# Attention on one core: the queries of eight heads loaded together in rows of 3 KB and put in place by GpSimd

## Chip, cores and metric

One core of a Trainium2 chip runs the kernel alone. The metric is the device time of one execution in microseconds (us), taken as the median of several executions. The engines are TensorE (PE; its weight loads are listed as PEld), VectorE (DVE), ScalarE (ACT), GpSimd (POOL) and SyncE (SP, which issues DMAs). DMA transfers run on 16 DMA engines that all queues share.

## What is computed

Softmax attention for 16 x 32 = 512 heads, each with 192 queries and 1024 keys of 128 numbers, all bf16:

```python
B, H, Sq, Sk, D = 16, 32, 192, 1024, 128
scale = q.shape[-1] ** -0.5
scores = jnp.einsum("bhqd,bhkd->bhqk", q, k) * scale
p = _softmax(scores, axis=-1)
return jnp.einsum("bhqk,bhkd->bhqd", p, v)
```

K and V are 134 MB each, Q and the output 25 MB each; every byte is moved once.

## The kernel before

**Tiling.** The heads are taken four at a time: 128 *quads*. Head a of a quad sits in partitions 32a to 32a+31, and its 128 contraction values are spread over these 32 partitions and four accumulating matmuls. The scores of a quad are computed transposed (keys on partitions) as 1536 columns: 8 key tiles of 192 queries. They are cut into three *steps* of 512 columns, so the program has NF = 384 steps f, with quad x = f // 3 and b = f % 3.

**One step.** TensorE computes QK of step f (line 654), then PV of step f-4 (line 683, `LAG = 4`). ScalarE takes the exp of head 0 (line 838) and of heads 1 to 3 (line 841) into `pt`. No maximum is subtracted. V has a column of ones beside it in `vp`, so PV gives the row sums too; VectorE takes their reciprocals (line 768) and multiplies (line 772) into `ob`. ScalarE's queue stores two quads at a time (line 522). A second, careful path stands behind a check of the row sums and isn't entered on this data.

**How Q, K and V get in place.** SP issues the loads, in an order written out by hand: for each n, V of quad n+3, K of quad n+5, Q of quad n+5. `load_k` (line 546) moves 128 rows of 8 KB, `load_v` (line 555) 512 rows of 2 KB, `load_q` (line 531) 128 rows of 1.5 KB (32 partitions per head, 6 query rows in each). K and V have five buffers each (`NKN`, `NVS`), and Q five (`qn`). SP waits until VectorE has turned K of quad n before it reuses the buffer, and until PV is done with V of quad n-2. The wait for K covers Q's buffer too.

VectorE turns K in three pieces per quad (`turn_k`, line 747) into `kx`, in 32 x 32 blocks of 4-byte words, three steps ahead (`AHEAD = 3`). GpSimd copies each piece into the order that TensorE reads (`order`, line 607, into `kt`). Q takes a shorter way: `turn_q` (line 756) turns it on VectorE with an output pattern that puts it in `qt` directly; it stands in VectorE's queue ahead of the K piece with b = 2. GpSimd also copies V into its padded place (`spread`, line 616), between the first and second K piece of the next quad. `qt`, `kt`, `vp` and `pt` have two buffers each, used in turn.

**Who waits for whom.** TensorE counts semaphores down (`take`). Ahead of QK it takes one of `s_kt` (GpSimd's K piece), one of `s_e1` (the exp that frees the scores' bank) and, at b = 0, one of `s_qt` (VectorE's Q). Ahead of PV it takes one of `s_on` (VectorE's last normalising step). V has no wait of its own in the loop: the K piece that follows `spread` in GpSimd's queue vouches for it.

Of the kernel before, what the change touches and what calls it, by code (L numbers as in the profile page):

```python
# [407 lines left out]
U32 = mybir.dt.uint32  # L408
# [12 lines left out]
def _attention_kernel(nc, q, k, v, out):  # L421
# [4 lines left out]
    NQ = NH // 4  # L426
    T = SK // 128
    scale = float(D) ** -0.5
    R = PE_LOOP
    assert NH % 8 == 0 and NQ >= 12  # L430
    NF = 3 * NQ
    LAG = 4
# [3 lines left out]

    AHEAD = 3
    NKN, NVS, NKT, NVP = 5, 5, 2, 2
    GQ = 2
    NSO = 3  # L440
    VB = 136
# [9 lines left out]
    with ExitStack() as outer:  # L451
# [7 lines left out]
        s_out = sem("f_out")  # L459
        s_blank = sem("f_blank")  # L460
        s_kn = [sem("f_kn%d" % i) for i in range(NKN)]
        s_qn = [sem("f_qn%d" % i) for i in range(NKN)]
        s_v = [sem("f_v%d" % i) for i in range(NVS)]
        s_st = [sem("f_st%d" % i) for i in range(NSO)]
        s_kx = sem("f_kx")
        s_qt = sem("f_qt")
        s_kt = sem("f_kt")
        s_vp = sem("f_vp")
        s_qk = sem("f_qk")
# [10 lines left out]
        with ExitStack() as es:  # L480
# [9 lines left out]
            kx = sb("f_kx", [128, 2, 2048], U32)  # L490

            kt = sb("f_kt", [128, NKT, 2 * T, 128, 2], BF16)
            qn = sb("f_qn", [128, NKN, 384], U32)

            qt = sb("f_qt", [128, R, 2, SQ, 2], BF16)
            vs = sb("f_vs", [128, NVS, 4, T * D], BF16)
# [32 lines left out]

            def load_q(e, x):  # L530
                e.dma_start(
                    qn[:, x % NKN, :],
                    qf[4 * x:4 * x + 4].rearrange("a (j u) d -> (a j) (u d)", u=6).bitcast(U32),
                ).then_inc(s_qn[x % NKN], 16)

            hints = {}

# [3 lines left out]
            @block.sync  # L541
            def _(e):
                def load_k(x, lo=0, hi=32):
                    if x >= NKN:
                        e.wait_ge(s_kx, 3 * (x - NKN) + 3)
                    e.dma_start(
                        kn[:, x % NKN, 64 * lo:64 * hi],
                        kf[4 * x:4 * x + 4].rearrange("a (j r) d -> (a j) r d", r=32)[:, lo:hi, :]
                        .rearrange("p r d -> p (r d)").bitcast(U32),
                    ).then_inc(s_kn[x % NKN], 16)  # L550

                def load_v(x, lo=0, hi=4):
                    if x >= NVS:
                        e.wait_ge(s_pv, 3 * (x - NVS) + 2 + BLANK)
                    e.dma_start(
                        vs[:, x % NVS, lo:hi, :],
                        vf[4 * x + lo:4 * x + hi].rearrange("a (m t) d -> m a (t d)", t=T),
                    ).then_inc(s_v[x % NVS], 16)


                load_k(0)
                e.wait_ge(s_blank, 1)
                load_k(1)
                load_q(e, 1)
                load_v(0, 0, 2)
                e.wait_ge(s_qk, PRE + 1)
                load_v(0, 2, 4)
                load_k(2, 0, 16)
                e.wait_ge(s_pv, BLANK - 2)
                load_k(2, 16, 32)  # L570
                load_q(e, 2)
                for n in range(3, NKN):
                    load_v(n - 2)
                    load_k(n)
                    load_q(e, n)
                for n in range(NQ):
                    if n == NQ // 2:
                        hint(e)
                    if n + NKN - 2 < NQ:
                        load_v(n + NKN - 2)  # L580
                    if n + NKN < NQ:
                        load_k(n + NKN)
                        load_q(e, n + NKN)
                for i in range(len(store_at), len(stores)):
                    store(e, i)
            def stored(e):
# [3 lines left out]
            @block.gpsimd  # L590
            def _(gp):
                gp.memset(ones[:], 1.0).then_inc(s_one, 1)  # L592

                def set_v(part):
                    return gp.memset(part.bitcast(U32), 0x3F803F80)  # L595

                set_v(vp[:, 0, 0:2 * T].rearrange("p a d -> p (a d)")).then_inc(s_set, 1)
                set_v(vp[:, 0, 2 * T:].rearrange("p a d -> p (a d)")).then_inc(s_blank, 1)
                set_v(vp[:, 1].rearrange("p a d -> p (a d)"))

                def order(g):
                    x, b = divmod(g, 3)
                    lo, hi = PIECES[b]
                    gp.wait_ge(s_kx, g + 1)
                    if x >= NKT - 1 and b == 0:
                        gp.wait_ge(s_qk, 3 * (x - NKT) + 3 + PRE)
                    gp.tensor_copy(  # L607
                        kt[:, x % NKT].bitcast(U32).rearrange("p U (j s u) c -> p U j s (u c)", s=2, u=2)[:, lo:hi],
                        kx[:, x % 2].rearrange("p (U s j u) -> p U j s u", s=2, j=32, u=2)[:, lo:hi],
                    ).then_inc(s_kt, 1)  # L610

                def spread(x, i):
                    if i == 0:
                        gp.wait_ge(s_v[x % NVS], 16 * (x // NVS + (2 if x % NVS == 0 else 1)))
                        gp.wait_ge(s_pv, 3 * (x - NVP) + 3 + BLANK)
                    gp.tensor_copy(  # L616
                        vp[:, x % NVP, 2 * T * i: 2 * T * i + 2 * T, 0:D].bitcast(U32),
                        vs[:, x % NVS, 2 * i: 2 * i + 2, :].rearrange("p a (t d) -> p (a t) d", d=D).bitcast(U32),
                    ).then_inc(s_vp, 1)

                for x in range(NQ + 1):
                    if x == NQ // 2:
                        hint(gp)
                    if x < NQ:
                        order(3 * x)
                    if x >= 1:
                        for i in range(2):
                            spread(x - 1, i)
                    if x < NQ:
                        order(3 * x + 1)  # L630
                        order(3 * x + 2)

            @block.tensor
            def _(pe):
# [3 lines left out]

                def qk(f):
                    x, b = divmod(f, 3)  # L640
                    if b == 0:
                        take(s_qt, 1)
                    take(s_kt, 1)
                    take(s_e1, 1)
                    ins = None
                    for group in CUTS[b]:
                        for w in range(4):
                            h, c = divmod(w, 2)
                            for g, (t, n0, n1) in enumerate(group):
                                c0 = t * SQ + n0 - 512 * b  # L650
                                for a in range(4):
                                    S = s3_ps[f % 2][:, a - 1, :] if a else s1_ps[:]
                                    r = slice(32 * a, 32 * a + 32)
                                    ins = pe.matmul(  # L654
                                        S[:, c0: c0 + n1 - n0],
                                        kt[r, x % NKT, 2 * t + h, :, c],
                                        qt[r, x % R, h, n0:n1, c],
                                        start=w == 0 and g == 0, stop=w == 3, skip_group_check=True,
                                        tile_position=(32 * a, 0))
                    ins.then_inc(s_qk, 1)  # L660
# [57 lines left out]
            def _(dve):  # L718
# [5 lines left out]
                    ins = clear(low[:, z, :, 1, :])  # L724
                ins.then_inc(s_set, 1)
                clear(qt[:, 1].rearrange("p h q c -> p (h q c)"))
                dve.sem_inc(s_e1, 1 + PRE)
                clear(kt[:, 1, 10:16].rearrange("p U k c -> p (U k c)")).then_inc(s_kt, 1)
                for z in range(2):
                    ins = clear(low[:, z, :, 2, :])  # L730
                ins.then_inc(s_out, 1)
                dve.wait_ge(s_out, 2)
                dve.wait_ge(s_blank, 1)
                dve.sem_inc(s_on, LAG + 1 + PRE)
                where = {}
                for i, (x0, c) in enumerate(stores):
                    for a in range(c):
# [2 lines left out]
                def turn_k(g):  # L740
# [8 lines left out]
                        kn[:, x % NKN].rearrange("p (s u U i) -> p s u U i", s=2, u=2, i=32)[:, :, :, lo:hi],  # L749
                    ).then_inc(s_kx, 1)  # L750

                def turn_q(x):
                    dve.wait_ge(s_qn[x % NKN], 16 * (x // NKN + 1))
                    if x >= R - 1:
                        dve.wait_ge(s_qk, 3 * (x - R) + 3 + PRE)
                    dve.transpose(  # L756
                        qt[:, x % R].bitcast(U32).rearrange("p b (y j u) c -> p u y b (j c)", y=3, u=2),
                        qn[:, x % NKN].rearrange("p (u y b i) -> p u y b i", u=2, y=3, b=2),
                    ).then_inc(s_qt, 1)

                def onorm(s):
                    x, w = divmod(s, 3)
# [35 lines left out]
                for f in range(NF + LAG + 1):  # L798
                    s = f - LAG - 1
                    if f == NF // 2:  # L800
                        hint(dve)
                    if s >= 0:
                        onorm(s)
                        if 0 <= s - EARLY < 3:
                            check(0, 2 * EARLY, 0, s - EARLY)
                    g = f + AHEAD
                    if 5 <= g < NF:
                        x, b = divmod(g, 3)
                        if b == 2 and x >= 2:
                            turn_q(x)  # L810
                        turn_k(g)
                for part in range(3):
                    check(2 * EARLY, 2 * NF, 1, part)
# [70 lines left out]
```

## Time and profile before

| what | value |
|---|---|
| median of 3 runs | 817.86 us (817.03 to 821.01) |
| profiled execution | 816.7 us, its span 815.0 us |
| granted TensorE clock | 0.996 |
| DMA over the span | 319.16 MB, mean 392 GB/s, 138455 packets (7217 under 512 B, 56369 under 2 KB) |
| ScalarE exps, lines 841 and 838 | 384 of 1444 ns and 384 of 597 ns |
| VectorE turns of K, line 747 | 256 of 972 ns (768 words), 128 of 670 ns (512 words) |
| VectorE turns of Q, line 756 | 128 of 570 ns (384 words) |
| GpSimd copies of K, line 607 | 256 of 863 ns (768 words), 128 of 642 ns (512 words) |
| GpSimd copies of V, line 616 | 256 of 1046 ns (1024 words) |
| issues of Q on SP, line 531 | 127, median 575 ns each |

The profile gives each engine's busy time over the span, and the groups of instructions by line, with the mean duration of one and the engine's idle time just before them. Busy times can overlap on one engine[...]. The *DMA share* is the time that packets took, as a share of 16 engines' time; the records of single packets lie in the trace. *Idle before* an instruction is put down to what released it last.

### The profile page before, as it was taken

What the parts mean: (1) busy time and instruction counts of PE and PEld (TensorE: products, weight loads), DVE (VectorE), ACT (ScalarE), POOL (GpSimd) and SP (SyncE); (2) the same over time, 40 slices, a digit from 0 to 9 for tenths busy, and PEclk for the clock granted to TensorE, in tenths of its full rate; (3) what the DMA queues carried; (4) which work ended last, traced back from release to release, by engine and by line L of the source; (5) the groups of instructions that cost most, each with busy time, mean ns of one, the idle gap of its engine ahead of it and who ended that gap; (6) DMA issues with size and microseconds to landing.
All of it is one profiled execution on the core that took longest, in us unless ns stands there. A gap on an engine that the chain in (4) does not pass through costs nothing. (4 is left out here: it accounts for less than half of the span.)

```text
span 815.0 us, 71454 instructions
## 1 busy us (share of the span) xinstructions
PE 802.2 (98%) x32996; PEld 716.0 (88%) x32996; DVE 602.0 (74%) x1293; ACT 749.9 (92%) x772; POOL 553.8 (68%) x648
## 2 busy tenths in 40 slices
PE   8899999999999999999999999999999999999997
PEld 7788888888888888888888888888888888888886
DVE  4677777777777777777777777777777777777775
ACT  6799999999999999999999999999999999999995
POOL 5677677667667766766676676676766766766674
PEclk9999999999999999999999999999999999999999
DMA  7999999999999999999999999999999999999992
GB/s 270 396 401 406 408 404 405 409 403 406 409 403 406 408 403 407 407 405 407 407 403 408 407 404 408 406 406 405 407 406 401 396 409 393 388 406 399 393 379 73
DMA packets 138455, 319.16 MB, mean 392 GB/s; under 512 B 7217, under 2 KB 56369, under 8 KB 122161
## 3 DMA queue, kind: packets, MB, share of 16 engines
q1 hardware_dynamic: 105536, 294.22, 91.9%
q10 hardware_dynamic: 32880, 24.58, 9.0%
q14 instruction: 33, 0.26, 0.1%
q8 instruction: 6, 0.10, 0.1%
HBM read 293.60 MB, written 25.17 MB: 391 GB/s over the span
## 5 line engine op out<-in xcount | busy, mean ns | idle before, releaser
L841 ACT ACTIVATE f_pt<-f_s 128x1536 bf16<-128x1536 f32 x384 | 554.6, 1444 | 0.1
L654 PE MATMUL f_s<-f_qt,f_kt 32*128 32x192 bf16 (+1 forms) x20528 | 423.2, 226 | 7.4 <-PEq L637 7.4
L683 PE MATMUL f_o<-f_vp,f_pt 128*64 128x129 bf16 x12368 | 426.8, 222 | 0.4 <-issue 0.2
L683 PEld LDWEIGHTS f_o<-f_vp,f_pt 128*64 128x64 bf16 x12368 | 363.7, 110 | 49.4 <-issue 22.5
L654 PEld LDWEIGHTS f_s<-f_qt,f_kt 32*128 32x128 bf16 x20528 | 349.4, 92 | 44.0 <-issue 9.1
L607 POOL COPY f_kt<-f_kx 128x768 uint32<-128x768 uint32 (+1 forms) x384 | 298.0, 789 | 112.6 <-DVE f_kx L747 110.3
L747 DVE STREAM_TRANSPOSE f_kx<-f_kn 128x768 uint32<-128x768 uint32 (+1 forms) x384 | 334.3, 871 | 38.4 <-DMA f_kn<-in_k_dram 36.5
L616 POOL COPY f_vp<-f_vs 128x1024 uint32<-128x1024 uint32 x256 | 260.1, 1046 | 137.8 <-DMA f_vs<-in_v_dram 129.7
L838 ACT ACTIVATE f_pt<-f_s 128x512 bf16<-128x512 f32 x384 | 229.3, 597 | 56.4 <-PE f_s L654 13.8
L768 DVE RECIPROCAL f_rinv<-f_o 128x2 f32<-128x2 f32 x381 | 64.2, 168 | 156.1 <-PE f_o L683 154.8
L772 DVE TENSOR_TENSOR f_ob<-f_o,f_rinv 128x256 bf16<-128x256 f32 x381 | 161.6, 424 | 13.3 <-DVE f_rinv L768 0.3
L756 DVE STREAM_TRANSPOSE f_qt<-f_qn 128x384 uint32<-128x384 uint32 x128 | 72.9, 570 | 0.0
L825 ACT ACTIVATE f_pt<-f_ones 128x1536 f32<-128x1536 bf16 x3 | 4.2, 1472 | 0.0
L595 POOL MEMSET f_vp<- 128x1088 uint32 (+1 forms) x3 | 3.8, 1312 | 0.0
L683 PE MATMUL f_s<-f_vp,f_pt 128*64 128x129 bf16 x96 | 3.2, 220 | 0.2 <-issue 0.2
L683 PEld LDWEIGHTS f_s<-f_vp,f_pt 128*64 128x64 bf16 x96 | 2.9, 110 | 0.5 <-issue 0.4
L825 ACT ACT_TABLE_LOAD x1 | 1.3, 1283 | 1.2 <-PEq L869 1.2
L696 PE MATMUL f_o<-f_ones 128*128 128x512 bf16 x2 | 1.0, 622 | 1.1 <-POOL f_ones L592 1.1
L720 DVE MEMSET f_pt<- 128x256 uint32 x4 | 1.1, 272 | 0.9 <-PEq L869 0.9
L768 DVE RECIPROCAL f_rinv<-f_s 128x2 f32<-128x2 f32 x3 | 0.5, 171 | 1.4 <-PE f_s L683 1.4
L713 PE MATMUL f_o<-f_bad,f_ones 128*1 128x1 bf16 x1 | 0.2, 165 | 1.3 <-DVEq L814 1.3
L713 PEld LDWEIGHTS f_o<-f_bad,f_ones 128*1 128x1 bf16 x1 | 0.1, 80 | 1.4 <-DVEq L814 1.4
(15 smaller groups left out, 6.8 us busy)
## 6 DMA issues: line engine op xcount, KB each, us to landing
f_kn<-in_k_dram SPq DMA_DIRECT2D x127, 1024.0 KB, 18.1
f_vs<-in_v_dram SPq DMA_DIRECT2D x127, 1024.0 KB, 16.3
f_qn<-in_q_dram SPq DMA_DIRECT2D x127, 192.0 KB, 14.2
out_dram<-f_ob ACTq DMA_DIRECT2D x62, 384.0 KB, 9.5
f_vs<-in_v_dram SPq DMA_DIRECT2D x2, 512.0 KB, 6.4
f_kn<-in_k_dram SPq DMA_DIRECT2D x2, 512.0 KB, 4.7
out_dram<-f_ob SPq DMA_DIRECT2D x1, 384.0 KB, 3.8
out_dram<-f_ob SPq DMA_DIRECT2D x2, 192.0 KB, 2.1
```

The source lines that it names most:

```text
L595: return gp.memset(part.bitcast(U32), 0x3F803F80)
L607: gp.tensor_copy(kt[:, x % NKT].bitcast(U32).rearrange("p U (j s u) c -> p U j s (u c)", s=2, u=2)[:, lo:hi], kx[:, x % 2].rearrange("p (U ...
L616: gp.tensor_copy(vp[:, x % NVP, 2 * T * i: 2 * T * i + 2 * T, 0:D].bitcast(U32), vs[:, x % NVS, 2 * i: 2 * i + 2, :].rearrange("p a (t d) ...
L654: ins = pe.matmul(S[:, c0: c0 + n1 - n0], kt[r, x % NKT, 2 * t + h, :, c], qt[r, x % R, h, n0:n1, c], start=w == 0 and g == 0, stop=w == 3 ...
L683: ins = pe.matmul(O[64 * z: 64 * z + 64, u, 0:129], pt[:, x % R, 2 * y + z, t * SQ + 64 * j: t * SQ + 64 * j + 64], vp[:, x % NVP, (2 * y ...
L747: dve.transpose(kx[:, x % 2].rearrange("p (U s j u) -> p s u U j", s=2, j=32, u=2)[:, :, :, lo:hi], kn[:, x % NKN].rearrange("p (s u U i) ...
L756: dve.transpose(qt[:, x % R].bitcast(U32).rearrange("p b (y j u) c -> p u y b (j c)", y=3, u=2), qn[:, x % NKN].rearrange("p (u y b i) -> ...
L768: dve.reciprocal(ri, O[:, :, 128]).then_inc(s_rc, 1)
L772: dve.tensor_tensor(ob[:, so, 6 * a + 2 * w: 6 * a + 2 * w + 2, :], O[:, :, 0:128], ri.unsqueeze(2).to_broadcast([128, 2, D]), ALU.mult,). ...
L825: return act.activation(part.bitcast(F32), ones[:, 0:1].to_broadcast([128, 2 * T * SQ // 2]), ACT_FN.Copy)
L838: act.activation(pt[:, x % R, 0, c], s1_ps[:], ACT_FN.Exp, scale=scale).then_inc(s_e1, 1)
L841: act.activation(pt[:, x % R, 1:4, c], s3_ps[f % 2][:], ACT_FN.Exp, scale=scale).then_inc(s_e3, 1)
```

## The change

Q is loaded for two quads at a time. Quads 0 and 1 keep their own loads and turns; from quad 2 on, `load_q2` issues four DMAs per pair of quads, one for each group of 32 partitions. Group a receives head a of both quads: partition 32a + 16h + j holds 12 query rows (3 KB) of that head in quad h of the pair. `qn` has three buffers of that size. In SP's order the four DMAs stand behind K of the even quad.

VectorE turns the whole 768-word tile once per pair (`turn_q2`) into a small tile `qx` with two buffers, ahead of the last K piece of the quad before the pair. GpSimd's `copy_q` picks each quad's half out of `qx` and writes `qt`; it stands in GpSimd's queue ahead of the quad's first K piece. TensorE no longer takes `s_qt`: since `copy_q` comes ahead of that K piece on GpSimd, `s_kt` vouches for Q as well. The first credits of `s_e1` and `s_on` are handed out by the two remaining `turn_q`, so that TensorE starts behind them.

```diff
+    NQN = 3
...
-            qn = sb("f_qn", [128, NKN, 384], U32)
+            qn = sb("f_qn", [128, NQN, 768], U32)
+            qx = sb("f_qx", [128, 2, 768], U32)
...
+            def load_q2(e, x):
+                y = x // 2
+                for a in range(4):
+                    e.dma_start(
+                        qn[32 * a:32 * a + 32, y % NQN, :],
+                        qf[4 * x:4 * x + 8].rearrange("(h a) (j u) d -> a h j (u d)", h=2, u=12)[a].bitcast(U32),
+                    ).then_inc(s_qn[y % NQN], 16)
...
                         load_k(n + NKN)
-                        load_q(e, n + NKN)
+                        if (n + NKN) % 2 == 0:
+                            load_q2(e, n + NKN)
...
+                def copy_q(x):
+                    gp.wait_ge(s_qx, x // 2)
+                    gp.wait_ge(s_qk, 3 * (x - R) + 3 + PRE)
+                    gp.tensor_copy(
+                        qt[:, x % R].bitcast(U32).rearrange("p b (y j v) c -> p b y j (v c)", y=3, v=4),
+                        qx[:, x // 2 % 2].rearrange("p (v y b h j) -> p h b y j v", v=4, y=3, b=2, h=2)[:, x % 2])
...
                     if x < NQ:
+                        if x >= 2:
+                            copy_q(x)
                         order(3 * x)
...
                     x, b = divmod(f, 3)
-                    if b == 0:
-                        take(s_qt, 1)
                     take(s_kt, 1)
...
+                def turn_q2(x):
+                    y = x // 2
+                    dve.wait_ge(s_qn[y % NQN], 64 * (y // NQN + (1 if y % NQN else 0)))
+                    if y >= 3:
+                        dve.wait_ge(s_qk, 3 * (x - 3) + 1 + PRE)
+                    dve.transpose(
+                        qx[:, y % 2], qn[:, y % NQN],
+                    ).then_inc(s_qx, 1)
...
-                        if b == 2 and x >= 2:
-                            turn_q(x)
+                        if b == 2 and x % 2 == 1 and x + 1 < NQ:
+                            turn_q2(x + 1)
                         turn_k(g)
```

More of the change, by code (lines that the diff above doesn't have):

```diff
@@ L461, in _attention_kernel @@
         s_kn = [sem("f_kn%d" % i) for i in range(NKN)]
-        s_qn = [sem("f_qn%d" % i) for i in range(NKN)]
+        s_q0 = [sem("f_q0%d" % i) for i in range(2)]
+        s_qn = [sem("f_qn%d" % i) for i in range(NQN)]
         s_v = [sem("f_v%d" % i) for i in range(NVS)]
@@ L465, in _attention_kernel @@
         s_kx = sem("f_kx")
-        s_qt = sem("f_qt")
+        s_qx = sem("f_qx")
         s_kt = sem("f_kt")
@@ L531, in load_q @@
                 e.dma_start(
-                    qn[:, x % NKN, :],
+                    qn[:, 0, 384 * x:384 * x + 384],
                     qf[4 * x:4 * x + 4].rearrange("a (j u) d -> (a j) (u d)", u=6).bitcast(U32),
-                ).then_inc(s_qn[x % NKN], 16)
+                ).then_inc(s_q0[x], 16)
+            def load_q2(e, x):
[5 more added lines that the diff above has]
+                    ).then_inc(s_qn[y % NQN], 16)
             hints = {}
@@ L570, in _ @@
                 load_k(2, 16, 32)
-                load_q(e, 2)
+                load_q2(e, 2)
                 for n in range(3, NKN):
@@ L574, in _ @@
                     load_k(n)
-                    load_q(e, n)
+                    if n % 2 == 0:
+                        load_q2(e, n)
                 for n in range(NQ):
@@ L726, in _ @@
                 clear(qt[:, 1].rearrange("p h q c -> p (h q c)"))
-                dve.sem_inc(s_e1, 1 + PRE)
+                dve.sem_inc(s_e1, PRE)
                 clear(kt[:, 1, 10:16].rearrange("p U k c -> p (U k c)")).then_inc(s_kt, 1)
@@ L733, in _ @@
                 dve.wait_ge(s_blank, 1)
-                dve.sem_inc(s_on, LAG + 1 + PRE)
+                dve.sem_inc(s_on, LAG - 1)
                 where = {}
@@ L752, in turn_q @@
                 def turn_q(x):
-                    dve.wait_ge(s_qn[x % NKN], 16 * (x // NKN + 1))
-                    if x >= R - 1:
-                        dve.wait_ge(s_qk, 3 * (x - R) + 3 + PRE)
+                    dve.wait_ge(s_q0[x], 16)
+                    if x == 1:
+                        dve.wait_ge(s_qk, PRE)
                     dve.transpose(
-                        qt[:, x % R].bitcast(U32).rearrange("p b (y j u) c -> p u y b (j c)", y=3, u=2),
-                        qn[:, x % NKN].rearrange("p (u y b i) -> p u y b i", u=2, y=3, b=2),
-                    ).then_inc(s_qt, 1)
+                        qt[:, x].bitcast(U32).rearrange("p b (y j u) c -> p u y b (j c)", y=3, u=2),
+                        qn[:, 0, 384 * x:384 * x + 384].rearrange("p (u y b i) -> p u y b i", u=2, y=3, b=2),
+                    ).then_inc(*((s_on, 2 + PRE) if x else (s_e1, 1)))
+                def turn_q2(x):
[6 more added lines that the diff above has]
+                    ).then_inc(s_qx, 1)
                 def onorm(s):
```

## The prediction

> **What bounds the kernel now.** I read the waits first, then the stretches, then the DMA part of the page. The chain of work that ended last covers only the final 9 us here and says nothing about the long middle.
>
> ```profile
> PE 802.2 (98%) x32996; PEld 716.0 (88%) x32996; DVE 602.0 (74%) x1293; ACT 749.9 (92%) x772; POOL 553.8 (68%) x648
> ...
> DMA  7999999999999999999999999999999999999992
> ...
> q1 hardware_dynamic: 105536, 294.22, 91.9%
> q10 hardware_dynamic: 32880, 24.58, 9.0%
> ```
>
> TensorE looks full, but so do the 16 DMA engines: their packets took 91.9 + 9.0 = 100.9% of the span. Over 100% is possible because neighbouring packets overlap slightly. The stretches give the steady value (columns: PE, PEld, DVE, ACT, POOL busy, clock, DMA share, GB/s):
>
> ```profile
> 100.00:300.00 200.00, 200.00 (x8320) 178.84 (x8318) 150.32 (x326) 188.85 (x196) 139.23 (x162) 1.00 1.04 406
> 300.00:500.00 200.00, 199.76 (x8316) 178.58 (x8304) 151.15 (x325) 188.56 (x195) 137.36 (x162) 1.00 1.04 406
> 500.00:700.00 200.00, 198.50 (x8235) 177.33 (x8228) 150.95 (x322) 187.02 (x195) 137.79 (x162) 1.00 1.04 403
> ```
>
> The share is 1.04 throughout, while TensorE's busy time sags from 200.00 to 198.50: it begins to wait. What for is in the list of waits:
>
> ```profile
> POOL f_vp L616 <- DMA f_vs<-in_v_dram: 129.7, 97, 3.1
> POOL f_kt L607 <- DVE f_kx L747: 110.3, 152, 3.0
> DVE f_kx L747 <- DMA f_kn<-in_k_dram: 36.5, 47, 5.7
> ```
>
> GpSimd waits for V from HBM 97 times; in the timeline there is no such wait at 102 us, 0.3 us of it at 251, and 2 to 3 us at 556 and 705. So the transfers are a hair slower than TensorE and eat up the buffers' lead. The issues agree:
>
> ```profile
> f_kn<-in_k_dram SPq DMA_DIRECT2D x127, 1024.0 KB, 18.1
> f_vs<-in_v_dram SPq DMA_DIRECT2D x127, 1024.0 KB, 16.3
> f_qn<-in_q_dram SPq DMA_DIRECT2D x127, 192.0 KB, 14.2
> ```
>
> K lands 18.1 us after its issue in the median, against 4.5 us at least: nearly three quads of data stand in the queues. DMA and TensorE are balanced within half a per cent (TensorE: one step per 2.055 us, the median distance of the first exps, so 6.165 us a quad). **Any engine time added to DMA goes straight into the total.**
>
> [...] the rows that queue q1 must move are 127x128 + 2x128 (K), 127x512 + 2x256 (V), 127x128 (Q), 512 + 2x256 (stores), together 99328; the page counts 105536 packets, and the 6208 left over are 16 for each of the 388 DMAs. No DMA of before has k under 16, so the small-k case isn't shown. [...]
>
> **The change, part by part.**
>
> *Packet prices.* The trace's packet records have nearly constant durations by size (median): 8192 B 309 ns, 2048 B 84, 1536 B 65, 768 B 36, a completion 9. With means (315.2, 86.2, 65.5, 36.1), one engine's work for one quad before is K 8 x 315.2 = 2522, V 32 x 86.2 = 2758, Q 8 x 65.5 = 524, output 16 x 36.1 = 578, completions 3.5 x 9 = 32: 6414 ns. Divided by the overlap 1.04 this is 6167 ns, the pace of the kernel. A row of 3072 B isn't in the trace; on the line through 2048 and 8192 B (0.0366 ns per byte) it takes 84 + 37.5 = 121.5, with the same excess of mean over median 122.5 ns. Bounds: 112.5 (no fixed part)[...].
>
> *Q's load: where the path is.* `load_q` takes 4 heads in one piece: 128 rows, outermost size 128. `load_q2` issues four DMAs per pair of quads; each reads [h=2][j=16] rows of 3072 B (h steps four heads, j one row, so the two don't merge) into 32 partitions. The outermost source dimension is 2, the destination's 32[...]. All of Q then runs on engines 0 and 1. Each gets 16 rows of each DMA, 64 per pair: 64 x 122.5 = 7840 ns, in place of 2 x 524 = 1048. Its whole work for a pair becomes K, V and output 2 x (2522 + 2758 + 578) = 11716, Q 7840, completions 9 x 9 = 81: 19637 ns, over 1.04 = 18.88 us. Before, a pair took 12.33 us. K and V are each spread over all 16 engines, and a load is complete only with its last engine's part, so everything moves at the pace of engines 0 and 1; the other 14 idle. Added: 6.55 us per pair, 63 pairs (the first two quads keep the old form): **+413 us**, all on the path. Buffers can't hide it, since it is a rate: five of K and V only set how much may be queued.
>
> *SP.* 252 Q issues in place of 126, at 0.575 us median: +72 us on SP's queue over the run. K's issue line already spends 379 us waiting on SP: covered, zero. If that cover were gone, 72 us spread over 63 pairs is 1.1 us each, still under a pair's 12.33.
>
> *VectorE.* Two turns of 570 ns per pair become one of 768 columns, bounded by K's 972 ns turn of that size above and half of it below; I take 0.97. It saves 0.17 us per pair, and VectorE is 74% busy: nothing. Behind its wait for Q stand the turn of K and the next normalising step, for which TensorE waits; Q is asked for five quads early, after K of the same quad and long before that quad's V would be used, so I expect V, not Q, to end the wait.
>
> *GpSimd.* One more copy per quad, 384 words: K's copies of 768 and 512 take 863 and 642 ns, so 0.863 ns a word and 0.53 us. Above: its source runs are 4 bytes; should that double the cost, 1.1 us. GpSimd works 2 x 863 + 642 + 2 x 1046 = 4460 ns of a quad's 6.17 us now and would work 4.99, or 5.5, of 9.4: hidden. Its new wait for TensorE is the one that `order` of the same quad has anyway; behind it are K's copy and V's spread.
>
> *TensorE.* The dropped wait costs nothing today: steps with it (402.20 to 404.25 us in the timeline) and without (404.25 to 406.31) are 2.05 and 2.06 us. Zero, and bounded by 128 x 0.01 us. Stalls do cost clock: after the gap before 27.02 us a step's QK took 1.90 us instead of 1.10 for one window. At such a pace throughout, a step's 2.055 us would become 3.53 (27.02 to 30.55) and a pair 21.2 us, more than 18.88; but the slow window lasted some 3.4 us, so one or two per pair add 1.4 to 2.8 us of TensorE time, and 6.5 us are free: zero, with the upper bound in the range.
>
> *Sum.* Profiled execution 816.7 us (span 815.0 and 1.7 around it) + 413 = 1229; the median of the three runs is 1.2 above it: **1230 us**.
>
> **Rivals.**
>
> [...] The others work about half of the time (11.3 us of a 21 us pair). If a Q packet goes at half rate meanwhile, Q's 7840 ns become 7840/0.74 = 10600, +2.65 us per pair, +167: **about 1395 us**. [...] Against it: the others may be done when Q's turn comes.
>
> *The split isn't what I read* (ends on the other side). If the hardware spreads each DMA over 16 engines, or rotates the pairs, each engine has 8 rows of 3 KB per pair: 980 + 36 in place of 1048 + 18, that is 50 ns less, 48 after overlap, -3 us: **815 us**. This is what larger rows are worth, and TensorE's 2.055 us per step caps it near there. It decides from k = 4 rotated or k of 16 upwards; a fixed k = 8 would still give 8 engines 1960 + 36 in place of 1066, +0.9 us a pair. For it: only that no DMA of before shows a small k.
>
> *GpSimd becomes the bound.* With k = 16 only: from 1.7 us per copy (6.17 - 4.46) it would set the pace; at 2 us each, +0.3 x 128 = 38, **856 us**. Against it: 4-byte runs would have to cost four times K's.
>
> **How the numbers follow.** Engines 0 and 1 full, plain: 0.58, at 1230. [...] Even spread: 0.13, at 815. GpSimd bound: 0.03, at 856. Something beyond 1400[...]: 0.04. The range runs from the bare packet price (64 x 10 ns less, over 1.04, by 63: -39, 1190)[...] and leaves out the even spread. A change under 0.5% can't be told from none here; the even spread straddles that at -0.4%: 0.08 same, 0.05 faster, 0.87 slower.
>
> **What would show it.** Completions: with k = 2 the Q loads post 504 in place of 2016, so packets under 512 B fall from 7217 to about 5700; with k = 16 they rise to about 9230. DMA's mean share falls to some 0.67 and GB/s to about 260 with the kernel still waiting on V; Q lands later than K; TensorE's busy share drops to about 66%, ScalarE's to about 61%. GpSimd's wait for V grows by some 400 us. If DMA stays at 1.04 and 400 GB/s, I am wrong about the split[...].

## The result, and the profile after

The changed kernel takes 1391.84 us (median, 1391.62 to 1395.27) against 818.13 us before: ratio 1.7013, 95% interval 1.6962 to 1.7064. The prediction named 1230 us, with a range of 1190 to 1400. The direction and the main cause were right; the size was 162 us short. Two of the experiments have executions over 1.5% above the fastest of their kernel; these are left out of comparisons.

Page of the changed kernel, parts 1 to 3 (busy time by engine; the DMA share and GB/s in 40 slices; packets; queues):

```profile
span 1393.5 us, 71577 instructions
...
PE 931.3 (67%) x32996; PEld 828.6 (59%) x32996; DVE 594.0 (43%) x1230; ACT 756.7 (54%) x772; POOL 653.1 (47%) x774
...
DMA  8768667676676766766767667667676675666763
...
DMA packets 128880, 319.17 MB, mean 229 GB/s; under 512 B 5704, under 2 KB 38728, under 8 KB 112584
...
q1 hardware_dynamic: 95960, 294.21, 62.3%
q10 hardware_dynamic: 32880, 24.58, 5.7%
```

The same bytes move, but the 16 engines are busy for only 68% of the span, and no compute engine is full either. The count of short packets settles how Q was split: they fell from 7217 to 5704. Among the records of queue q1 the completions (4 bytes) fell from 6208 to 4696, by the 2016 - 504 = 1512 that k = 2 asked for (k is the number of engines that carry one DMA, read here from its completions; the packets in flight, below, agree). Four DMAs per pair post eight completions, two each.

The waits of the changed kernel:

```profile
POOL f_kt L623 <- DVE f_kx L771: 701.0, 191, 14.9
...
DVE f_qx L792 <- DMA f_qn<-in_q_dram: 469.9, 63, 17.3
ACT f_pt L876 <- PE f_o L707: 450.2, 62, 9.4
PE f_o L707 <- PEq L663: 441.6, 62, 9.3
...
POOL f_vp L639 <- DMA f_vs<-in_v_dram: 1.6, 1, 1.6
```

Once per pair (63 times) VectorE stands before Q's turn; behind it in its queue stand K's last piece and the normalising step, so GpSimd, TensorE and ScalarE stop with it. V, for which GpSimd waited 129.7 us before, is now early: 1.6 us.

Stretches of one period, alternately quiet and full, of the changed kernel (columns: length, busy PE, PEld, DVE, ACT, POOL, clock, DMA share, GB/s):

```profile
612.50:620.30 7.80, 5.58 (x164) 5.10 (x168) 4.88 (x10) 3.21 (x3) 5.08 (x6) 0.59 0.22 86
620.30:634.00 13.70, 8.68 (x360) 7.59 (x348) 4.29 (x10) 8.53 (x10) 5.08 (x6) 0.95 0.99 332
634.00:641.90 7.90, 5.63 (x180) 5.04 (x182) 5.41 (x11) 3.39 (x3) 5.09 (x6) 0.66 0.15 56
641.90:655.50 13.60, 8.19 (x336) 7.27 (x334) 4.19 (x10) 8.35 (x9) 5.08 (x6) 0.91 0.98 319
```

A pair takes 21.5 us. For nearly 8 of them the share is around 0.15 to 0.22, where two of sixteen engines at work give 0.125. The records of single packets show the same: over the stretch from 200 to 1300 us, exactly two packets are in flight for 29.6% of the time and fewer than two for 0.2%. That fits two engines that never rest and fourteen that do; the records don't name the engines.

Two more things can be read there. First, the two engines are out of step: one does its 64 rows of Q in 8.2 us, mostly in the quiet stretch, while the other does K and V; then, 1.4 us later, the other does its 64 rows in 10.3 us, mostly while all engines are busy. They did not start like that. In the first pair all 128 rows pass within 11.0 us, at 169 ns a packet; over the first eleven pairs, up to about 240 us, the two runs move apart. A pair took 20.9 us then, so being out of step is not what makes it long. Second, a Q packet takes 121 to 122 ns where it is undisturbed, as worked out, but 141.3 in the mean, and the disturbance has a pattern: in the first engine's run the mean of most rows is 122 to 126 ns, and the rows that stand out are mainly rows 8 to 10, in the first and in the second DMA:

```text
mean ns of row 0..15 of the first engine's Q (50 pairs)
DMA 1: 146 143 122 121 122 122 122 123 124 188 199 124 124 127 126 124
DMA 2: 124 122 123 124 125 124 124 124 202 245 210 124 124 124 124 124
DMA 3: 124 122 122 124 125 125 126 123 124 123 123 123 124 124 125 123
DMA 4: 124 124 125 124 128 134 123 126 124 125 126 125 126 135 138 128
```

There, a packet takes up to twice as long (245 ns in place of 124). The rows stay the same ones over 50 pairs while the addresses in HBM move on with each pair, which speaks against the addresses that are read. Whether it is the place where these rows are written (the records give no addresses) or the moment within the pair at which they pass was not shown. In the second engine's run, with all engines busy, many more rows stand out.

### The profile page after: what moved, and what is told of

Same layout as the page of the kernel before. It is cut to its first block, busy times and chain, and to the rows that moved or that the text cites. A ratio compares the mean times of both kernels' runs of the same rounds, so it can differ in the third digit from the quotient of the medians.

```text
span 1393.5 us, 71577 instructions
## 1 busy us (share of the span) xinstructions
PE 931.3 (67%) x32996; PEld 828.6 (59%) x32996; DVE 594.0 (43%) x1230; ACT 756.7 (54%) x772; POOL 653.1 (47%) x774
## 2 busy tenths in 40 slices
DMA packets 128880, 319.17 MB, mean 229 GB/s; under 512 B 5704, under 2 KB 38728, under 8 KB 112584
## 5 line engine op out<-in xcount | busy, mean ns | idle before, releaser
L707 PE MATMUL f_o<-f_vp,f_pt 128*64 128x129 bf16 x12368 | 504.5, 244 | 441.9 <-PEq L663 441.6
L707 PEld LDWEIGHTS f_o<-f_vp,f_pt 128*64 128x64 bf16 x12368 | 436.6, 125 | 498.0 <-issue 482.4
L678 PE MATMUL f_s<-f_qt,f_kt 32*128 32x192 bf16 (+1 forms) x20528 | 471.8, 242 | 15.6 <-PEq L663 13.5
L678 PEld LDWEIGHTS f_s<-f_qt,f_kt 32*128 32x128 bf16 x20528 | 389.1, 99 | 61.8 <-issue 29.4
L792 DVE STREAM_TRANSPOSE f_qx<-f_qn 128x768 uint32<-128x768 uint32 x63 | 61.6, 978 | 469.9 <-DMA f_qn<-in_q_dram 469.9
L631 POOL COPY f_qt<-f_qx 128x384 uint32<-128x384 uint32 x126 | 109.9, 872 | 0.0
```

Source lines behind the costliest of these rows:

```text
L631: gp.tensor_copy(qt[:, x % R].bitcast(U32).rearrange("p b (y j v) c -> p b y j (v c)", y=3, v=4), qx[:, x // 2 % 2].rearrange("p (v y b h ...
L678: ins = pe.matmul(S[:, c0: c0 + n1 - n0], kt[r, x % NKT, 2 * t + h, :, c], qt[r, x % R, h, n0:n1, c], start=w == 0 and g == 0, stop=w == 3 ...
L707: ins = pe.matmul(O[64 * z: 64 * z + 64, u, 0:129], pt[:, x % R, 2 * y + z, t * SQ + 64 * j: t * SQ + 64 * j + 64], vp[:, x % NVP, (2 * y ...
L792: dve.transpose(qx[:, y % 2], qn[:, y % NQN],).then_inc(s_qx, 1)
```

## The experiments

The edits are shown against the changed kernel, unless said otherwise; the counts in VectorE's wait for Q, which follow the number of DMAs, are left out.

**All of the change but the shape of its loads.**

```diff
-                for a in range(4):
-                    e.dma_start(
-                        qn[32 * a:32 * a + 32, y % NQN, :],
-                        qf[4 * x:4 * x + 8].rearrange("(h a) (j u) d -> a h j (u d)", h=2, u=12)[a].bitcast(U32),
+                for h in range(2):
+                    e.dma_start(
+                        qn[:, y % NQN, 384 * h:384 * h + 384],
+                        qf[4 * x + 4 * h:4 * x + 4 * h + 4].rearrange("a (j u) d -> (a j) (u d)", u=6).bitcast(U32),
...
-                        qx[:, x // 2 % 2].rearrange("p (v y b h j) -> p h b y j v", v=4, y=3, b=2, h=2)[:, x % 2])
+                        qx[:, x // 2 % 2].rearrange("p (h v y b j) -> p h b y j v", v=2, y=3, b=2, h=2)[:, x % 2])
```

> All of the change but the shape of the load: two DMAs per pair, each of 128 partitions in rows of 1.5 KB, as before; one turn per pair into the small tile, GpSimd's copy and TensorE without its wait stay. Theory (the loss is the transfers' rate on two engines): the 16 engines carry Q evenly again, so 818, within 0.5% of before; 8 packets of 65 ns per quad and engine as before. Rival (the loss is the new waits: VectorE waits for Q of a whole pair, GpSimd has a copy more): still clearly slower than before, over 850, with VectorE waiting for Q by some 100 us or more.

819.07 us against 817.99: ratio 1.0009, interval 0.9997 to 1.0020. In this kernel VectorE turns Q per pair, GpSimd copies it and TensorE has no own wait for it, and that costs and gains nothing that can be measured. Its waits:

```profile
POOL f_kt L623 <- DVE f_kx L771: 179.5, 241, 3.7
...
DVE f_qx L792 <- DMA f_qn<-in_q_dram: 13.4, 8, 6.6
```

The wait for Q is the same instruction in the same place, but it falls from 469.9 us to 13.4. So neither the place of the wait nor the order of issue is the cause: all of the 574 us lies in the four DMAs and their shape.

**Sixteen engines, rows of 3 KB, eight DMAs of 16 partitions.**

```diff
                 for a in range(4):
-                    e.dma_start(
-                        qn[32 * a:32 * a + 32, y % NQN, :],
-                        qf[4 * x:4 * x + 8].rearrange("(h a) (j u) d -> a h j (u d)", h=2, u=12)[a].bitcast(U32),
-                    ).then_inc(s_qn[y % NQN], 16)
+                    for h in range(2):
+                        e.dma_start(
+                            qn[32 * a + 16 * h:32 * a + 16 * h + 16, y % NQN, :],
+                            qf[4 * x + 4 * h + a].rearrange("(j u) d -> j (u d)", u=12).bitcast(U32),
+                        ).then_inc(s_qn[y % NQN], 16)
```

> The change with eight DMAs of 16 partitions per pair (one per head) in place of four with an outer dimension of 2: each DMA runs on 16 engines, one row of 3 KB each. [...] 8 x (490 - 122) = 2.9 us per pair and engine, times 63 = +185, about 1000 at most; packets of 3072 B well above 122 ns. Theory without sharing (rate on two engines alone): 815, packets at 122 ns.

911.88 us, ratio 1.1141 (1.1108 to 1.1173): 480 us of the loss are gone with the two engines, but it isn't 815. Stretches of this kernel:

```profile
100.00:300.00 200.00, 179.78 (x7432) 160.26 (x7429) 133.74 (x276) 170.40 (x176) 146.63 (x174) 1.00 1.04 365
300.00:500.00 200.00, 178.77 (x7213) 159.33 (x7211) 128.97 (x269) 165.04 (x169) 142.45 (x170) 0.97 1.04 353
```

The DMA share is 1.04 as before the change, that is full, but at 353 to 365 GB/s in place of 406: every packet takes longer. Q's have a mean of 163 ns, and K's have grown from 315 to 347 and V's from 86 to 98.6. One engine's work for a pair is then K 16 x 346.8 + V 64 x 98.6 + Q 8 x 163 + output 32 x 36.5 + completions 13 x 11.2 = 14477 ns, over 1.04 = 13.92 us. The packets are those of the profiled execution, which took 920.87 us: 12.33 + 102.9 / 63 = 13.96 us a pair. So the longer packets account for the time. K and V, which nobody touched, carry some 0.5 and 0.8 us of the addition; Q itself loses only 0.3 against its 122 ns. The 490 ns that the expectation allowed a packet, four times its 122, were its author's estimate and were not seen.

**Sixteen engines, two rows of each DMA per engine.**

```diff
-                        qf[4 * x:4 * x + 8].rearrange("(h a) (j u) d -> a h j (u d)", h=2, u=12)[a].bitcast(U32),
+                        qf[4 * x:4 * x + 8].rearrange("(h a) (j u) d -> a j h (u d)", h=2, u=12)[a].bitcast(U32),
...
-                        qx[:, x // 2 % 2].rearrange("p (v y b h j) -> p h b y j v", v=4, y=3, b=2, h=2)[:, x % 2])
+                        qx[:, x // 2 % 2].rearrange("p (v y b j h) -> p h b y j v", v=4, y=3, b=2, h=2)[:, x % 2])
```

> The change with the rows of each of the four DMAs in the order row, quad (outer dimension 16 in place of 2), and GpSimd's copy reading accordingly: each DMA runs on 16 engines, two rows each[...]. [...] 8 x 122 = 1.0 us per pair and engine, +62 at most: 815 to 880[...]. Without sharing: 815[...].

924.94 and 928.58 us, 1.13 times before (the median of all four executions is 935.31 us; recorded ratio 1.1431, 1.1330 to 1.1532). Only the order of two dimensions differs from the change, and it is some 465 us faster. The short packets fit k = 16:

```profile
DMA packets 132408, 319.18 MB, mean 346 GB/s; under 512 B 9232, under 2 KB 42256, under 8 KB 116112
```

But the expectation of 815 to 880 us was missed: I had taken this version for the faster of the two, an estimate that no trace had shown, and it isn't. Q's packets take 172.8 ns, K's 346.6, V's 98.4, close to those of the version before. Why it is no faster than the version before stays open. The number of DMAs doesn't explain it either: this version has four per pair, that one eight.

**Half of Q on the two engines** (from quad 8 on, each row loads its first 1.5 KB only, and the rest of the tile keeps older queries).

```diff
+                    w = 768 if y <= 3 else 384
                     e.dma_start(
-                        qn[32 * a:32 * a + 32, y % NQN, :],
-                        qf[4 * x:4 * x + 8].rearrange("(h a) (j u) d -> a h j (u d)", h=2, u=12)[a].bitcast(U32),
+                        qn[32 * a:32 * a + 32, y % NQN, 0:w],
+                        qf[4 * x:4 * x + 8].rearrange("(h a) (j u) d -> a h j (u d)", h=2, u=12)[a, :, :, 0:2 * w].bitcast(U32),
```

> The change as it is, but from quad 8 on each row loads only its first 1.5 KB; the second half of Q's tile keeps what an earlier pair left there, so those queries are wrong. The number of DMAs, of packets and of engines stays. Theory (rate of two engines): 64 packets of some 65 to 75 ns in place of 141, 4.2 to 4.9 us less per pair, 60 pairs: 250 to 290 less, so 1100 to 1140. Rival (the four issues, or the latency of the last-issued load, set the pace): little changes, over 1330.

1087.4 us (ratio 1.3290, interval 1.3250 to 1.3329): 304 us less for the same number of DMAs, packets and waits, and somewhat below the 1100 to 1140 expected. The wait for Q is less than half of the changed kernel's:

```profile
DVE f_qx L793 <- DMA f_qn<-in_q_dram: 224.5, 63, 18.2
```

That is 5.07 us per pair, or 79 ns per row of Q for the 1.5 KB left out, where the packet prices alone say 122.5 - 65.5 = 57. Q's packets fell by 141.3 - 72.5 = 69 ns in the mean, which is 4.4 of the 5.07 us; the rest wasn't traced. So the time follows the bytes on the two engines, and more than the undisturbed packets would say.

**Rows of 3 KB in one DMA over 128 partitions** (the heads get each other's queries).

```diff
-                for a in range(4):
-                    e.dma_start(
-                        qn[32 * a:32 * a + 32, y % NQN, :],
-                        qf[4 * x:4 * x + 8].rearrange("(h a) (j u) d -> a h j (u d)", h=2, u=12)[a].bitcast(U32),
-                    ).then_inc(s_qn[y % NQN], 16)
+                e.dma_start(
+                    qn[:, y % NQN, :],
+                    qf[4 * x:4 * x + 8].rearrange("a (j u) d -> (a j) (u d)", u=12).bitcast(U32),
+                ).then_inc(s_qn[y % NQN], 16)
```

> The change with one DMA per pair over all 128 partitions, 3 KB rows taken straight on through the eight heads: 16 engines[...]. The rows land in other partitions than the change puts them, so the heads get each other's queries; sizes, counts and all work are those of the change. [...] 3072 B packets at 121 to 123 ns, K and V back at 315 and 86 ns in the mean, and the time is what larger rows are worth: 815, at most 819. Rival (3 KB rows are slow to read or to write by themselves): packets above 140 ns and a time near the 912 of the version with sixteen engines.

813.92 us against 817.01: ratio 0.9959 (0.9943 to 0.9975), and this is the only kernel of the study that is faster than before. Q's packets take 121.9 ns, K's 314.7, V's 85.8: none is longer than worked out (122.5) or than before (315.2 and 86.2). Stretches of this kernel:

```profile
300.00:500.00 200.00, 200.00 (x8320) 178.94 (x8318) 148.51 (x308) 188.84 (x196) 165.15 (x195) 1.00 1.04 408
500.00:700.00 200.00, 200.00 (x8315) 178.77 (x8312) 149.25 (x311) 188.82 (x195) 164.66 (x195) 1.00 1.04 406
```

TensorE's busy time stays at 200.00, where it sagged to 198.50 before: the transfers no longer fall behind, and TensorE's own pace is the floor. So 3 KB rows, loaded in one DMA per pair, are a small gain (0.4%), and they are not slow by themselves. Against this kernel the version with sixteen engines in small slices loses 98 us, with rows of the same size. One difference between the two is the number of DMAs (one in place of eight per pair). They may also differ in which rows an engine reads and where it writes them, which the records don't show; no run changes one of these alone.

**Rows of 1.5 KB in sixteen DMAs of 16 partitions per pair** (the first experiment of this section, in slices).

```diff
                 for h in range(2):
-                    e.dma_start(
-                        qn[:, y % NQN, 384 * h:384 * h + 384],
-                        qf[4 * x + 4 * h:4 * x + 4 * h + 4].rearrange("a (j u) d -> (a j) (u d)", u=6).bitcast(U32),
-                    ).then_inc(s_qn[y % NQN], 16)
+                    for w in range(8):
+                        e.dma_start(
+                            qn[16 * w:16 * w + 16, y % NQN, 384 * h:384 * h + 384],
+                            qf[4 * x + 4 * h + w // 2].rearrange("(j u) d -> j (u d)", u=6)[16 * (w % 2):16 * (w % 2) + 16].bitcast(U32),
+                        ).then_inc(s_qn[y % NQN], 16)
```

> Rows of 1.5 KB with 16 engines, but in sixteen DMAs of 16 partitions per pair[...]; everything else as in the version with small rows and two DMAs, which took 819. [...] Q's packets above 65 ns, K and V above 315 and 86, and a loss of the order of the 94 us of the 3 KB rows in the same pattern[...]: 860 to 920. Rival (3 KB rows are the cause): 819, within 1%, up to some 5 us for the 14 further completions per pair and engine (14 x 9 ns x 63 = 8 us before overlap).

972.99 us, ratio 1.1891 (1.1851 to 1.1932). The rival falls: the same 1.5 KB rows that cost nothing in two DMAs cost 154 us in sixteen. Q's packets take 84.9 ns in the mean in place of 65.6, V's 104 in place of 86, K's 334 in place of 316. The loss is above what I expected. One engine's work for a pair is 16 x 333.9 + 64 x 104 + 16 x 84.9 + 32 x 36.9 + 21 x 9.6 = 14739 ns; the share is 0.99 here in most stretches, not 1.04, which gives 14.9 us, and the profiled execution (976.96 us) took 12.33 + 160 / 63 = 14.9. So the packets explain the time, but part of it is the overlap that was lost. What took the overlap (the number of DMAs, the engines losing step) wasn't separated.

## Why the prediction was right, and where it wasn't

*DMA and TensorE balanced; DMA time goes straight into the total.* Right as far as the longer packets go: in the version with eight DMAs the sum over packets gives 13.92 us a pair, measured 13.96. The forecast of -3 us for evenly spread rows came out at -3.1 in the version with one DMA per pair, but that agreement is partly luck. With one completion per pair and engine in place of four, the same working saves 82 ns, not 50, and gives -5 us; TensorE, busy for 200.00 of 200 us, ends the gain sooner.

*k = 2, Q on two engines.* Right, and it is the cause: completions fell by the 1512 forecast, two packets are in flight for 30% of the time, half of Q's bytes make 304 us of difference, and a change of order in the dimensions (k = 16) takes some 465 us off. No trace of before showed a DMA on two engines, since each DMA of that kernel posted 16 completions; the prediction took it as given. Here outermost sizes of 2 and 32 gave two completions per DMA, 504 for 252 DMAs. Which two engines these are isn't shown, since the records don't name engines; 0 and 1 in the prediction are no more than names for two of them.

*6.55 us per pair.* This term was too small: 21.5 - 12.33 = 9.1 us were measured, 2.6 more. The prediction put 0.58 on packets at their undisturbed price and 0.22 on the rival at 1395, in which a Q packet goes at half rate while the other engines work; that half was its author's estimate, and no trace of before showed it. The step that failed is the argument against the rival: that the others may be done when Q's turn comes. The later of the two engines shows the parts. Its Q run takes 10.3 us: 64 packets with a mean of 146 ns, 9.35 (1.5 more than at 122.5), and the output's 32 packets of 36 ns in between, 1.15, with next to no overlap. My sum had (7.84 + 1.15) / 1.04 = 8.64 for this. The rest of its pair takes 11.2 us for K, V and completions, where it had 10.64 / 1.04 = 10.2. So some 1.5 of the missing 2.6 us is Q's packets taking longer; the remaining 1.1 lies in the overlap of 1.04 by which I had divided, and in K and V stretched by others or not overlapped (over all engines, K's mean packet rose from 315 to 382 ns and V's from 86 to 97.6). The rival's 1395 met the measured 1392, but its working put all 2.65 us on Q's packets (166 ns); they took 141 over both engines. So the nearness of 1395 to 1392 is in part luck, and the measured time lies 8 us under the upper end of the range, which was there for this rival. A version with two engines and undisturbed packets wasn't run, so the split of the 2.6 is read from the packets, not shown by an experiment. That the form of Q's loads slows other transfers is shown: K's and V's packets, the same in size and number, take 347 and 98.6 ns at 912 us, and 314.7 and 85.8 at 814. Where they meet is not shown: the place of writing, the number of DMAs and the reading side aren't separated.

*"I expect V, not Q, to end the wait."* Wrong. V's wait fell to 1.6 us and Q's rose to 469.9. Q is issued behind K of its own quad and needed at once with it; V of that quad is issued two quads later but needed only three to four steps on, and two quads' worth of data comes between. With one Q run of 8 to 10 us per pair on each of the two engines, Q is what arrives last. The total doesn't depend on which one it is, since a rate sets it.

*SP, VectorE, GpSimd, TensorE at zero.* Right for the last three together: 819.07 against 817.99. SP's four issues per pair aren't in that version, which has two. In the changed kernel the four take SP 7.6 and 8.3 us (at 609 and 630 us of the timeline), not the 2.3 of my prices; with half of Q's bytes they still take 6.8 to 8.7 us (at 610 and 628 us), at 304 us less, so they don't set the pace. The turn takes 978 ns (0.97 taken). GpSimd's copy takes 872, not 530; the range to 1.1 us held, and at 81% busy in the fastest version it is still hidden:

```profile
L792 DVE STREAM_TRANSPOSE f_qx<-f_qn 128x768 uint32<-128x768 uint32 x63 | 61.6, 978 | 469.9 <-DMA f_qn<-in_q_dram 469.9
...
L631 POOL COPY f_qt<-f_qx 128x384 uint32<-128x384 uint32 x126 | 109.9, 872 | 0.0
```

The lines are the changed kernel's; with the small rows, where the copy gathers from two places in place of four, it takes 591 ns.

*The clock.* Right that it isn't the bound. TensorE stands for about 7 us per pair. Its granted clock falls to half in the stall (0.50 from 612.1 to 618.9 us) and stays there for the first 3 to 4 us of work (from 614.72 us), so it is 0.819 over the span:

```profile
606.96 1.10 PE L678 MATMUL f_s<-f_qt,f_kt 32*128 32x192 bf16 x48
614.72 1.94 PE L707 MATMUL f_o<-f_vp,f_pt 128*64 128x129 bf16 x32 [6.66 <-PEq L663]
616.59 1.90 PE L678 MATMUL f_s<-f_qt,f_kt 32*128 32x64 bf16 x64
618.42 1.32 PE L707 MATMUL f_o<-f_vp,f_pt 128*64 128x129 bf16 x32
619.67 1.09 PE L678 MATMUL f_s<-f_qt,f_kt 32*128 32x128 bf16 x48
```

In this timeline (start, duration, operation, idle before) the slow steps cost some 2 us per pair and are over long before Q's next landing at 634 us.

## What to carry to other kernels

Before a load is reshaped for longer rows, write down both access patterns with the outermost dimension first: here an outermost size of 2 left two engines at work, and the order of two dimensions decided between 1392 and some 927 us. Then compare with one load over all 128 partitions, like the big loads beside it: here it took 814 us, and the same rows in slices of 16 partitions 912, with K and V slowed too (347 and 98.6 ns a packet in place of 314.7 and 85.8). What in the slices slows them was not shown. Packets with nearly fixed prices (medians of 84 ns for 2048 B both before and after the change, 309 and 316 for 8192 B) make such a sum easy, and the count of the shortest packets (5704 in place of 7217) showed on the page how many engines took part.

## What the runs showed of the hardware that was not expected

- Q in slices of 16 partitions slowed transfers that have nothing to do with it: K's mean packet rose from 315 to 347 ns and V's from 86 to 98.6 for 8 rows of Q per pair and engine. The same rows in one DMA over 128 partitions left them at 314.7 and 85.8.
- The two engines of a DMA need not work side by side: they began together, and after about 240 us one ran its 64 rows while the other was still at K and V, and the second followed 1.4 us after the first had ended.
- Four DMAs of 32 partitions per pair were no better than eight of 16, with rows of 3 KB on sixteen engines (925 to 929 us and 911 to 921), and the version with sixteen small DMAs per pair lost the overlap of packets (share 0.99 in place of 1.04).
- In the changed kernel the granted clock is at half for 6.8 us in 43 of 65 stretches and for 10.2 us in 19, part of it within the stall of about 7 us. Before the change, the stretch after the stall of 2.2 us that ended at 27.02 us lasted 3.4 us.
